# A decayed-attention and two-MoE kernel on one core: attention blocks loaded four ahead, weights' pieces one a block, decay tables made in turn

## Chip, core and metric

The kernel runs on one core of one Trainium2 chip. The metric is device time in microseconds (us) of one execution. Times stand as the median of the runs; the profile is one execution apart from them.

## What is computed

```python
def reference(q, k, v, moe_w_in, moe_w_out, moe2_w_gate, moe2_w_val, moe2_w_out):   # q, k, v: 2 x 8 x 768 x 64
    gamma = 1 - 2.0 ** (-5 - arange(8))
    for t in range(768):                               # retention: a linear attention with decay
        state = gamma * state + outer(k[t], v[t])
        y[t] = q[t] @ state / 8
    x = y as 1536 tokens x 512
    h = x @ moe_w_in                                   # 512 x 2048
    x = (h * tanh(log1p(exp(h)))) @ moe_w_out          # 2048 x 512
    return (sigmoid(x @ moe2_w_gate) * (x @ moe2_w_val)) @ moe2_w_out   # 512 x 1536, 1536 x 512
```

All is fp32 in and out. The weights come as 64-bit words.

## The kernel before

**Attention** runs over 12 blocks of 128 tokens (`NSUB`; 6 of each sequence, `SPB`). Of each block `load(j)` (L449) brings q and k, features first, in one transfer (`qk_t`, 512 KB), and k and v, tokens first, in another (`nv_t`, 512 KB), into rings of three buffers (`ld`, L440). `at_scores(j)` (L461) makes the scores on PE (16 matmul passes into two PSUM banks `sc`), the scaled values `vp` on POOL, and on DVE the two masked scores `a`. `fin(j)` (L518) is `at_state`, which adds the block to the state `st` and lets ACT copy it to `s` for the next block, and `at_out`, which forms the output `ao` from `a` and `vp` and, but for the first block of a sequence, from `s`. DVE then writes `ao` times a decay table `og` into `acc` (L498). The table of a block's place in its sequence is made by POOL from the first one (L473) in the first sequence, kept in six tiles and used again in the second.

**Dense work.** Four blocks are a chunk of 512 tokens. PE multiplies numbers that were split into a high and a low part, three matmuls for each product (`mm3`, L105). So each operand is first split by `split` (L88): ACT copies the high part, DVE or POOL subtracts for the low one. The first chunk's operand is `xc`, made by `put_plain` (L222), the second's are `B11` and `B21`, made by `put_block` (L226): four ACT copies and four DVE differences of 128x512 each. `plain1` (L393) gives dense steps of 12 matmuls with N = 512 on these operands; behind each Mish on ACT and the split of its result `g` (difference on POOL).

**Weights.** A piece is 512 KB (`raw`, three buffers, `stg`). `load_piece` (L129) issues the next one; `pump` (L202) takes the next step of a plan: decode a piece (`decode`, L92: one ACT step, then a TENSOR_SCALAR and two SCALAR_TENSOR_TENSOR on DVE) and `put` it (L158), which copies the high part on ACT and appends the low part's difference to the list `late`; the next pump or the next `weight` empties that list. One dense step calls one pump behind it (`seq`, L379).

**Order.** Until `early.clear()` (L555) every engine follows the order in which the program is written (`InOrder`, L52, records the calls; hence L65 on the profile's rows of this part). Behind it a scheduler orders the instructions. The part in program order is:

```python
for j in range(j0, j0 + SPC):
    if j + 1 < NSUB:
        at_scores(j + 1)
    fin(j)
    load(j + 3)
    load_piece()
    if dense:
        dense.pop(0)()
    if j < SPC:
        pump()
```

once over blocks 0 to 3 with no dense steps, then `put_plain()`, then over blocks 4 to 7 with four dense steps of the first chunk, then `put_block` twice, then over blocks 8 to 11 with the four dense steps of the second chunk (L548 to L554). Ahead of it three blocks and two pieces are loaded (L543 to L547). Behind it come `out1_first` (L403), the sums of operands (L230), and the main loops over weight pairs.

Of the kernel before, what the change touches and what calls it, by code (L numbers as in the profile page):

```python
# [9 lines left out]
F32 = mybir.dt.float32  # L10
# [4 lines left out]
ALU = mybir.AluOpType  # L15
PSUM = bass.MemoryType.PSUM

P = 128
# [4 lines left out]
def kernel(ctx, tc, qk, nv, w1i, w1o, w2g, w2v, w2o, ma_in, og_in, sg_in, ck_in, out):  # L23
# [14 lines left out]
    NP = KK  # L38
    D = P // 2
# [4 lines left out]
    SPC = N // P  # L44
    SPB = NSUB // 2
    RING = 10
    STG = 3
    WARM = 6

    early = [True]  # L50

# [19 lines left out]
    pe, dve, act, pool, sync = [InOrder(e) for e in (nc.tensor, nc.vector, nc.scalar, nc.gpsimd, nc.sync)]  # L71
# [14 lines left out]
    acc_t = [big.tile([P, KK, N], F32, name=f"acc{c}") for c in range(NCH)]  # L86
# [31 lines left out]
    for j in range(FF2 // 2):  # L118
        f = 2 * j
# [6 lines left out]
    steps, late, sums_t, vs = [], [], {}, {}  # L126
    lo_eng = {"w": dve, "g": pool}

    def load_piece():  # L129
        n = cnt["dma"]  # L130
        if n >= len(pieces) or n >= cnt["raw"] + STG:
            return
        kind, i = pieces[n]
        t = stg.tile([P, DM], I64, tag="raw", name="raw")
        sync.dma_start(out=t, in_=src[kind][i])
        raws.append(t)
        cnt["dma"] += 1
# [61 lines left out]
                    ("s", *key, n), sums_t[key][:, 2 * n:2 * n + 2].rearrange("p a b -> p (a b)"))))  # L199
        return True  # L200

    def pump(n=1):  # L202
        while late:
            late.pop(0)()
        for _ in range(n):
            if not steps and not plan():
                return
            if steps[0][0] and not room() or steps[0][0] == 0 and "dcs" not in lo_eng:
                return
            steps.pop(0)[1]()  # L210

    def weight(key):
        while key not in w_t:
            if not steps:
                assert plan(), key
            steps.pop(0)[1]()
        while late:
            late.pop(0)()
        return w_t[key]


    def put_plain():  # L222
        for kk in range(KK):
            split(acc_t[0][:, kk], xc_t[:, kk, 0], xc_t[:, kk, 1], dve)

    def put_block(n, c, k0, eng=None):  # L226
        for k in range(2):
            split(acc_t[c][:, k0 + k], b_t[n][:, k, 0], b_t[n][:, k, 1], eng or dve)
# [150 lines left out]
    def seq(ss, end=None):  # L379

        def step(n):
            ss[n]()
            if n == len(ss) - 1 and end:
                end()
            pump()

        return [lambda n=n: step(n) for n in range(len(ss))]

# [4 lines left out]
    def plain1(i, c=0):  # L393
        ss, r = plain_steps((1, i), (None, ("B11", "B21"), ("T4", "B22"))[c])

        def end(m):
            if m and c == 2:
                dead.update({("a", 1, i, 0), ("a", 1, i, 1)})
            mish(r["c"][m], (1, 2 * i + m, c))

        return [f for m in range(2) for f in seq([ss[m]], lambda m=m: end(m))]
# [35 lines left out]

    with ExitStack() as actx:
        ac = actx.enter_context(tc.tile_pool(name="ac", bufs=1))
        ld = actx.enter_context(tc.tile_pool(name="ld", bufs=3))  # L440
        at = actx.enter_context(tc.tile_pool(name="at", bufs=2))
        ps_s = actx.enter_context(tc.tile_pool(name="ps_s", bufs=1, space=PSUM))
        ma = ac.tile([P, 1, P], F32, name="ma")
        ck = ac.tile([P, SPB, 2 * NP, 1], F32, name="ck")
        sg = ac.tile([P, SPB, NP, 1], F32, name="sg")
        og = [ac.tile([P, NP, P], F32, name=f"og{b}") for b in range(SPB)]
        qk_t, nv_t, a_t, vp_t, st_t, s_t = {}, {}, {}, {}, {}, {}

        def load(j):  # L449
            if j < NSUB:  # L450
                qk_t[j] = ld.tile([P, 2, NP, P], F32, tag="qk", name="qk_t")
                sync.dma_start(out=qk_t[j], in_=qk[j])
                nv_t[j] = ld.tile([P, 2, 2 * NP, D], F32, tag="nv", name="nv_t")
                sync.dma_start(out=nv_t[j], in_=nv[j])
                if j == 0:
                    sync.dma_start(out=ck, in_=ck_in)
                    sync.dma_start(out=ma, in_=ma_in)
                    sync.dma_start(out=og[0], in_=og_in)
                    sync.dma_start(out=sg, in_=sg_in)

        def at_scores(j):  # L461
            t = qk_t[j]
            sc = [ps_h.tile([P, NP, P], F32, tag="h", name="sc") for _ in range(2)]
            for p in range(NP):
                for e in range(2):
                    r = slice(D * e, D * e + D)
                    pe.matmul(out=sc[e][:, p, :], lhsT=t[r, 1, p, :], rhs=t[r, 0, p, :])
            vp_t[j] = at.tile([P, 2 * NP, D], F32, tag="vp", name="vp")
            pool.tensor_tensor(
                out=vp_t[j], in0=nv_t[j][:, 1], in1=ck[:, j % SPB].to_broadcast([P, 2 * NP, D]), op=ALU.mult  # L470
            )
            if 0 < j < SPB:
                pool.tensor_tensor(out=og[j], in0=og[0], in1=sg[:, j].to_broadcast([P, NP, P]), op=ALU.mult)  # L473
            a = at.tile([P, 2, NP, P], F32, tag="a", name="a")
            for e in range(2):
                dve.tensor_tensor(out=a[:, e], in0=sc[e], in1=ma.to_broadcast([P, NP, P]), op=ALU.mult)
            a_t[j] = a

        def at_out(j):
            a, v, t, s = a_t.pop(j), vp_t[j], qk_t[j], s_t.get(j)  # L480
            o = ps_o.tile([P, NP, P], F32, tag="o", name="ao")
            inter = j % SPB > 0

            for p in range(NP):
                for e in range(2):
                    pe.matmul(
                        out=o[D * e:D * e + D, p, :], lhsT=v[:, 2 * p + e, :], rhs=a[:, e, p, :],
                        start=p == 0, stop=p == NP - 1 and not inter, skip_group_check=True,
                    )
            if inter:  # L490
                for p in range(NP):
                    for e in range(2):
                        r = slice(D * e, D * e + D)
                        pe.matmul(
                            out=o[r, p, :], lhsT=s[r, p, :], rhs=t[r, 0, p, :], start=False, stop=p == NP - 1,
                            skip_group_check=True,
                        )
            dve.tensor_tensor(  # L498
                out=acc_t[j // SPC][:, :, j % SPC * P:j % SPC * P + P], in0=o, in1=og[j % SPB], op=ALU.mult
            )  # L500

        def at_state(j):
            if j % SPB == SPB - 1:
                return
            v, k = vp_t[j], nv_t[j]
            if j % SPB == 0:
                st_t[0] = ps_s.tile([P, NP, D], F32, tag="s", name="st")
            st = st_t[0]
            for p in range(NP):
                for e in range(2):  # L510
                    pe.matmul(
                        out=st[D * e:D * e + D, p, :], lhsT=k[:, 0, 2 * p + e, :], rhs=v[:, 2 * p + e, :],
                        start=j % SPB == 0 and p == 0, stop=p == NP - 1, skip_group_check=True,
                    )
            s_t[j + 1] = at.tile([P, NP, D], F32, tag="s", name="s")
            act.activation(out=s_t[j + 1], in_=st, func=AF.Copy)

        def fin(j):  # L518
            at_state(j)
            at_out(j)  # L520

        def blocks(j0, dense):

            for j in range(j0, j0 + SPC):
                if j + 1 < NSUB:
                    at_scores(j + 1)
                fin(j)
                load(j + 3)
                load_piece()
                if dense:  # L530
                    dense.pop(0)()
                if j < SPC:
                    pump()
            run(dense)

        dve.memset(ap=one_t, constant=1.0)
        act.activation(out=sig, in_=one_t, func=AF.Mish)
        z = ac.tile([P, NP * D], F32, name="z")
        dve.memset(ap=z, constant=0.0)
        for n in range(WARM):  # L540
            o = ps_o.tile([P, NP * D], F32, tag="o", name="warm")
            pe.matmul(out=o, lhsT=z[:, 0:P], rhs=z)
        load(0)  # L543
        load(1)
        load(2)
        load_piece()
        load_piece()  # L547
        at_scores(0)  # L548
        blocks(0, [])
        put_plain()  # L550
        blocks(SPC, plain1(0) + plain1(1))
        put_block("B11", 1, 0)
        put_block("B21", 1, 2)
        blocks(2 * SPC, plain1(0, 1) + plain1(1, 1))  # L554
        early.clear()  # L555

    big2 = ctx.enter_context(tc.tile_pool(name="big2", bufs=1))
    up = ctx.enter_context(tc.tile_pool(name="up", bufs=4))
# [35 lines left out]
    for j in range(NG):  # L594
        f = 2 * j
# [62 lines left out]
```

## Time and profile before

| | |
|---|---|
| median of 3 runs | 609.68 us (607.5 to 610.08) |
| the profiled execution | 610.06 us, of which its span is 608.3 |
| busy PE, DVE, POOL, ACT | 587.5 us (97%), 420.3 (69%), 325.2 (53%), 249.8 (41%) |
| mean granted clock of PE | 0.989 |
| chain that ended last | PE 74%, DVE 16%, DMA 2%, ACT 2%, POOL 2%, issue 2% |
| moved by DMA | 52.27 MB, mean 86 GB/s |

Times on rows are in us from the span's start unless marked ns. An engine's row tells in brackets how long it sat idle before it and what ended that. PE's passes are counted: an fp32 matmul of the attention part is two instructions. A granted clock of 1.00 is 2.4 GHz, 0.50 is 1.2 GHz; a mean between them is time at either.

### The profile page before, as it was taken

To read this page: it belongs to the slowest core of one execution; us is meant where nothing else is said; L and a number is where in the kernel's file an instruction comes from. 1 tells how busy PE (TensorE), PEld (TensorE's weight loads), DVE (VectorE), ACT (ScalarE), POOL (GpSimd) and SP (SyncE) were. 2 spreads that over 40 slices of the span, in tenths; PEclk is the share of its full clock that TensorE was granted. 3 is DMA by queue.
4 is the path that set the end of the run, shared out by engine and by line. 5 is a ranking of instruction groups with operands and counts; after the bars stand their busy time and mean duration, and the time that the engine had idled before them with its cause. 6 is when DMAs were issued, how large, how long until landed. Compare 5 with 4: busy or idle time off the path is not lost.

```text
span 608.3 us, 7961 instructions
## 1 busy us (share of the span) xinstructions
PE 587.5 (97%) x3056; PEld 480.6 (79%) x3056; DVE 420.3 (69%) x572; ACT 249.8 (41%) x433; POOL 325.2 (53%) x263
## 2 busy tenths in 40 slices
PE   7789899999999999998999999999999999999997
PEld 6667688888788788886788787888888888888885
DVE  3978799409786676746775985687487587473554
ACT  1243454445454452452434645642334343333210
POOL 3424149326877665574741567755467557457200
PEclk9889899999999999998999999999999999999999
DMA  9866322103231213312021022233023123100014
GB/s 346 324 248 216 139 70 78 62 1 105 73 101 56 84 34 105 105 35 69 36 69 36 1 70 70 70 103 103 1 71 99 41 69 104 35 1 1 1 52 157
DMA packets 15591, 52.27 MB, mean 86 GB/s; under 512 B 1984, under 2 KB 2112, under 8 KB 15552
## 3 DMA queue, kind: packets, MB, share of 16 engines
q1 hardware_dynamic: 15552, 51.75, 24.9%
q8 instruction: 24, 0.39, 0.3%
q14 instruction: 15, 0.12, 0.1%
HBM read 48.60 MB, written 3.15 MB: 85 GB/s over the span
## 4 chain that ended last, share of the span: by engine, by line
PE 74%; DVE 16%; DMA 2%; ACT 2%; POOL 2%; issue 2%; SPq 0%; DVEq 0%; ACTq 0%
PE o L108 31%; PE h L108 28%; PE hx L108 7%; PE h L65 4%; DVE v L101 3%; PE ao L65 2%; DVE v L102 2%; DVE v L100 2%; DVE acc L354 2%; DMA qk_t<-qk 2%; DVE v L65 1%; PE sc L65 1%; POOL w L162 1%; POOL g L90 1%; DVE T L90 1%
## 5 line engine op out<-in xcount | busy, mean ns | idle before, releaser
L90 POOL TENSOR_TENSOR g<-e,g 128x512 fp32r<-128x512 f32 x72 | 103.1, 1441 | 83.4 <-ACT g L89 83.4
L108 PE MATMUL o<-g,w 128*128 128x512 f32 x576 | 141.3, 394 | 2.9 <-DVE acc L354 2.7
L108 PEld LDWEIGHTS o<-g,w 128*128 128x128 f32 x576 | 108.6, 190 | 28.2 <-DVE acc L354 5.0
L108 PE MATMUL h<-T,w 128*128 128x512 f32 x444 | 112.3, 390 | 1.0 <-DVE T L90 0.6
L162 POOL TENSOR_TENSOR w<-v,w 128x512 fp32r<-128x512 f32 x56 | 76.2, 1369 | 67.2 <-ACT w L161 67.0
L108 PE MATMUL o<-w,g 128*128 128x512 f32 x432 | 106.0, 389 | 0.0
L108 PEld LDWEIGHTS h<-T,w 128*128 128x128 f32 x444 | 83.2, 188 | 19.4 <-DVE T L90 1.0
L108 PEld LDWEIGHTS o<-w,g 128*128 128x128 f32 x432 | 81.0, 188 | 17.1 <-POOL g L90 0.4
L108 PE MATMUL h<-B,w 128*128 128x512 f32 x336 | 87.8, 390 | 0.8 <-DVE e L344 0.8
L354 DVE TENSOR_TENSOR acc<-o,acc 128x512 f32<-128x512 f32 x72 | 49.1, 686 | 38.4 <-PE o L108 38.1
L108 PEld LDWEIGHTS h<-B,w 128*128 128x128 f32 x336 | 62.9, 188 | 14.4 <-DVE e L344 1.2
L89 ACT ACTIVATE g<-e 128x512 fp32r<-128x512 f32 x76 | 47.6, 631 | 52.6 <-DVE e L344 35.1
L162 POOL TENSOR_TENSOR w<-s,w 128x512 fp32r<-128x512 f32 x34 | 47.9, 1415 | 35.2 <-ACT w L161 35.0
L374 DVE TENSOR_TENSOR acc<-o,acc 128x512 f32<-128x512 f32 x60 | 41.1, 687 | 30.7 <-PE o L108 30.3
L161 ACT ACTIVATE w<-v 128x512 fp32r<-128x512 f32 x58 | 36.1, 630 | 62.6 <-DVE v L102 34.7
L100 DVE TENSOR_SCALAR v<-v 128x512 int32<-128x512 int32 x58 | 44.4, 767 | 23.2 <-ACT v L99 22.9
L99 ACT ACTIVATE v<-raw 128x512 f32<-128x512 f32 x58 | 38.6, 670 | 49.7 <-POOL w L162 20.0
L102 DVE SCALAR_TENSOR_TENSOR v<-raw,v 128x512 int32<-128x512 int32 x58 | 57.0, 984 | 0.5
L101 DVE SCALAR_TENSOR_TENSOR v<-raw,v 128x512 int32<-128x512 int32 x58 | 56.4, 973 | 1.1
L108 PE MATMUL hx<-xc,w 128*128 128x512 f32 x216 | 55.6, 389 | 0.0
L108 PE MATMUL h<-xc,w 128*128 128x512 f32 x216 | 54.8, 389 | 0.0
L108 PEld LDWEIGHTS hx<-xc,w 128*128 128x128 f32 x216 | 40.6, 188 | 8.4
(78 smaller groups left out, 632.8 us busy)
## 6 DMA issues: line engine op xcount, KB each, us to landing
raw<-w1i SPq DMA_DIRECT2D x16, 512.0 KB, 3.4
raw<-w1o SPq DMA_DIRECT2D x16, 512.0 KB, 3.8
qk_t<-qk SPq DMA_DIRECT2D x12, 512.0 KB, 4.4
nv_t<-nv SPq DMA_DIRECT2D x12, 512.0 KB, 5.5
raw<-w2g SPq DMA_DIRECT2D x12, 512.0 KB, 3.3
raw<-w2v SPq DMA_DIRECT2D x12, 512.0 KB, 3.4
raw<-w2o SPq DMA_DIRECT2D x12, 512.0 KB, 3.4
out<-acc SPq DMA_DIRECT2D x12, 256.0 KB, 2.0
```

Of the source, the lines that this page charges most:

```text
L65: i = call(**kw)
L89: act.activation(out=hi, in_=raw, func=AF.Copy)
L90: eng.tensor_tensor(out=lo, in0=raw, in1=hi.bitcast(F32), op=ALU.subtract)
L99: act.activation(out=v, in_=high.bitcast(F32), func=AF.Copy, scale=2.0 ** -112)
L100: dve.tensor_scalar(out=b, in0=b, scalar1=3, scalar2=None, op0=ALU.logical_shift_left)
L101: dve.scalar_tensor_tensor(out=b, in0=low, scalar=29, in1=b, op0=ALU.logical_shift_right, op1=ALU.bitwise_or)
L102: dve.scalar_tensor_tensor(out=b, in0=high, scalar=SIGN, in1=b, op0=ALU.bitwise_and, op1=ALU.bitwise_or)
L108: pe.matmul(out=o, lhsT=w(a), rhs=x(b), start=first and n == 0, stop=last and n == 2, skip_group_check=more)
L161: act.activation(out=hi, in_=v, func=AF.Copy)
L162: late.append(lambda: lo_eng["w"].tensor_tensor(out=lo, in0=v, in1=hi.bitcast(F32), op=ALU.subtract))
L354: dve.tensor_tensor(out=acc, in0=o, in1=acc, op=ALU.add)
L374: dve.tensor_tensor(out=acc, in0=o, in1=acc, op=ALU.add)
```

## The change

Four attention blocks are loaded ahead in place of three blocks and two pieces, into rings of four buffers (`AHEAD`). In a block the order becomes: next scores, `pump` (from block 3 on), `fin`, `load`, `load_piece`, at a chunk's last block the making of the next chunk's operand (`made`), the low part of the weight (`flush`), the dense step. A dense step of the ordered part no longer pumps. The decay tables other than the first are made by POOL in both sequences, into a ring of two (`og_t`), and the warm-up operand `z` lies in a ring's buffer.

```diff
+    AHEAD = 4
...
+    def flush():
         while late:
             late.pop(0)()
+
+    def pump(n=1):
+        flush()
...
-            pump()
+            if not early:
+                pump()
...
-        ld = actx.enter_context(tc.tile_pool(name="ld", bufs=3))
+        ld = actx.enter_context(tc.tile_pool(name="ld", bufs=AHEAD))
...
-        og = [ac.tile([P, NP, P], F32, name=f"og{b}") for b in range(SPB)]
+        og0 = ac.tile([P, NP, P], F32, name="og0")
...
-            if 0 < j < SPB:
-                pool.tensor_tensor(out=og[j], in0=og[0], in1=sg[:, j].to_broadcast([P, NP, P]), op=ALU.mult)
+            og_t[j] = og0
+            if j % SPB:
+                og_t[j] = at.tile([P, NP, P], F32, tag="og", name="og")
+                pool.tensor_tensor(out=og_t[j], in0=og0, in1=sg[:, j % SPB].to_broadcast([P, NP, P]), op=ALU.mult)
...
-        def blocks(j0, dense):
+        def blocks(j0, dense, made):
 
             for j in range(j0, j0 + SPC):
                 if j + 1 < NSUB:
                     at_scores(j + 1)
+                if j >= SPC - 1:
+                    pump()
                 fin(j)
-                load(j + 3)
+                load(j + AHEAD)
                 load_piece()
+                if j == j0 + SPC - 1:
+                    made()
+                flush()
                 if dense:
                     dense.pop(0)()
-                if j < SPC:
-                    pump()
             run(dense)
...
-        z = ac.tile([P, NP * D], F32, name="z")
+        z = at.tile([P, NP * D], F32, tag="s", name="z")
...
-        load(0)
-        load(1)
-        load(2)
-        load_piece()
-        load_piece()
+        for j in range(AHEAD):
+            load(j)
         at_scores(0)
-        blocks(0, [])
-        put_plain()
-        blocks(SPC, plain1(0) + plain1(1))
-        put_block("B11", 1, 0)
-        put_block("B21", 1, 2)
-        blocks(2 * SPC, plain1(0, 1) + plain1(1, 1))
-        early.clear()
+        blocks(0, [], put_plain)
+        blocks(SPC, plain1(0) + plain1(1), lambda: (put_block("B11", 1, 0), put_block("B21", 1, 2)))
+        blocks(2 * SPC, plain1(0, 1) + plain1(1, 1), early.clear)
```

On SP the transfers that follow block 1's stood so before (`qk_t` and `nv_t` are an attention block's two transfers, `raw` a weight's piece):

```order
L65 DMA qk_t_139<-qk 128x1024
L65 DMA nv_t_141<-nv 128x1024
L65 DMA raw_143<-w1i 128x512
L65 DMA raw_145<-w1i 128x512
L65 DMA qk_t_199<-qk 128x1024
L65 DMA nv_t_201<-nv 128x1024
L65 DMA raw_203<-w1i 128x512
L65 DMA qk_t_256<-qk 128x1024
```

and stand so now:

```order
L66 DMA qk_t_134<-qk 128x1024
L66 DMA nv_t_136<-nv 128x1024
L66 DMA qk_t_138<-qk 128x1024
L66 DMA nv_t_140<-nv 128x1024
L66 DMA qk_t_195<-qk 128x1024
L66 DMA nv_t_197<-nv 128x1024
L66 DMA raw_199<-w1i 128x512
L66 DMA qk_t_246<-qk 128x1024
```

The first piece moved from behind block 2 to behind block 4, and one piece stands between two blocks from there on.

On DVE, from block 4's masked scores to the first operand `xc` and block 5's masked scores, before (`v` is a decoded piece, `w` a weight's low part):

```order
L65 TENSOR_TENSOR a_341<-sc_328,ma_102 128x512
L65 TENSOR_TENSOR a_341<-sc_329,ma_102 128x512
L65 TENSOR_TENSOR acc0_87<-ao_354,og3_108 128x4x128
L65 TENSOR_TENSOR w_326<-v_321,w_326 128x512
L65 TENSOR_SCALAR v_379<-v_379 128x512
L65 SCALAR_TENSOR_TENSOR v_379<-raw_260,v_379 128x512 x2
L65 TENSOR_TENSOR xc_86<-acc0_87,xc_86 128x512 x4
L65 TENSOR_TENSOR a_407<-sc_394,ma_102 128x512
```

and now:

```order
L66 TENSOR_TENSOR a_317<-sc_303,ma_102 128x512
L66 TENSOR_TENSOR a_317<-sc_304,ma_102 128x512
L66 TENSOR_SCALAR v_320<-v_320 128x512
L66 SCALAR_TENSOR_TENSOR v_320<-raw_199,v_320 128x512 x2
L66 TENSOR_TENSOR acc0_87<-ao_337,og_264 128x4x128
L66 TENSOR_TENSOR xc_86<-acc0_87,xc_86 128x512 x4
L66 TENSOR_TENSOR w_325<-v_320,w_325 128x512
L66 TENSOR_TENSOR a_384<-sc_370,ma_102 128x512
```

The decode moved from between `acc` and `xc` to ahead of `acc`, and the weight's low part from ahead of `xc` to behind it.

On ACT, around the second operand, before (`e` is Mish, `g` the copy of its result, `v` a decode's first step, `w` a weight's high part, `s` the state's copy):

```order
L65 ACTIVATE s_626<-st_550 128x256
L65 ACTIVATE e_666<-h_652 128x512
L65 ACTIVATE g_668<-e_666 128x512
L65 ACTIVATE v_671<-raw_507 128x512
L65 ACTIVATE w_676<-v_671 128x512
L65 ACTIVATE B11_84<-acc1_88 128x512 x2
L65 ACTIVATE B21_85<-acc1_88 128x512 x2
L65 ACTIVATE s_709<-st_550 128x256
```

and now:

```order
L66 ACTIVATE v_599<-raw_426 128x512
L66 ACTIVATE w_604<-v_599 128x512
L66 ACTIVATE s_614<-st_536 128x256
L66 ACTIVATE B11_84<-acc1_88 128x512 x2
L66 ACTIVATE B21_85<-acc1_88 128x512 x2
L66 ACTIVATE e_662<-h_649 128x512
L66 ACTIVATE g_664<-e_662 128x512
L66 ACTIVATE v_684<-raw_491 128x512
L66 ACTIVATE w_689<-v_684 128x512
L66 ACTIVATE s_699<-st_536 128x256
```

The copies of `B11` and `B21` moved from behind block 7's Mish and decode to ahead of them, and a block's state copy now stands behind its weight copy.

## Rows read from the trace of the kernel before

**Rows 1.** Stretches: us; busy PE, PEld, DVE, ACT, POOL; granted clock; DMA share; GB/s

```profile
38.00:60.12 22.12, 22.12 (x261) 18.05 (x260) 18.50 (x24) 9.55 (x17) 9.70 (x8) 0.98 0.62 217
62.86:67.50 4.64, 4.64 (x14) 3.17 (x14) 4.64 (x8) 1.78 (x4) 0.00 (x0) 0.66 0.56 225
```

**Rows 2.** Waits of PE, 85.4 us to the end: total us, times, longest

```profile
PE o L108 <- DVE acc L354: 2.7, 3, 2.3
```

**Rows 3.** Time line of PE, blocks 1 to 4: start, us, what, idle before

```profile
13.07 1.09 PE L65 MATMUL ao<-qk_t,s 64*64 64x128 f32 x16
17.08 1.16 PE L65 MATMUL sc<-qk_t 64*128 64x128 f32 x16 [2.92 <-DMA qk_t<-qk]
...
22.27 1.16 PE L65 MATMUL sc<-qk_t 64*128 64x128 f32 x16
...
24.85 1.09 PE L65 MATMUL ao<-qk_t,s 64*64 64x128 f32 x16
...
29.95 1.09 PE L65 MATMUL ao<-qk_t,s 64*64 64x128 f32 x16
```

**Rows 4.** Time line, the first operand and the first two dense products

```profile
32.62 2.18 ACT L65 ACTIVATE xc<-acc 128x512 fp32r<-128x512 f32 x4
33.27 2.50 DVE L65 TENSOR_TENSOR xc<-acc,xc 128x512 fp32r<-128x512 f32 x4 [1.22 <-ACT xc L65]
...
33.29 0.50 PE L65 MATMUL h<-xc,w 128*128 128x512 f32 x1 [2.24 <-ACT xc L65]
...
34.01 4.02 PE L65 MATMUL h<-xc,w 128*128 128x512 f32 x11 [0.23 <-DVE xc L65]
...
41.43 3.01 PE L65 MATMUL h<-xc,w 128*128 128x512 f32 x12
```

**Rows 5.** Time line of PE, the second operand's first product

```profile
62.86 4.63 PE L65 MATMUL h<-B,w 128*128 128x512 f32 x12 [2.74 <-ACT B L65]
```

**Rows 6.** Time line, transfers issued by SP and what they released

```profile
6.95 0.39 SPq L65 DMA_DIRECT2D qk_t<-qk  x1
...
10.48 0.97 PEld L65 LDWEIGHTS sc<-qk_t 64*128 64x128 f32 x16 [0.17 <-DMA qk_t<-qk]
...
13.02 0.67 ACT L65 ACTIVATE v<-raw 128x512 f32<-128x512 f32 x1 [2.91 <-DMA raw<-w1i]
```

**Rows 7.** DMA issues between 5 and 10 us: KB, us to landing

```profile
qk_t<-qk SPq DMA_DIRECT2D x1, 512.0 KB, 10.0
```

**Rows 8.** Groups by form, 38 to 60.12 us: busy us, mean ns, idle before

```profile
L65 DVE SCALAR_TENSOR_TENSOR v<-raw,v 128x512 int32<-128x512 int32 x7 | 7.7, 1105 | 0.2
L65 DVE TENSOR_SCALAR v<-v 128x512 int32<-128x512 int32 x4 | 4.2, 1051 | 3.4 <-ACT v L65 3.4
L65 DVE TENSOR_TENSOR a<-sc,ma 128x512 f32<-128x512 f32 x6 | 3.8, 682 | 0.0
L65 DVE TENSOR_TENSOR acc<-ao,og 128x512 f32<-128x512 f32 x3 | 2.0, 680 | 0.0
...
L65 ACT ACTIVATE w<-v 128x512 fp32r<-128x512 f32 x3 | 1.9, 632 | 9.9 <-DVE v L65 9.9
L65 ACT ACTIVATE s<-st 128x256 f32<-128x256 f32 x2 | 0.7, 366 | 0.0
```

**Rows 9.** Time line of POOL and DVE, 10 to 16 us

```profile
10.21 1.04 POOL L65 TENSOR_TENSOR og<-og,sg 128x512 f32<-128x512 f32 x1
...
13.72 0.46 DVE L65 TENSOR_SCALAR v<-v 128x512 int32<-128x512 int32 x1 [2.43 <-ACT v L65]
14.21 1.42 DVE L65 SCALAR_TENSOR_TENSOR v<-raw,v 128x512 int32<-128x512 int32 x2
```

**Rows 10.** Time line behind the blocks, 90 to 140 us

```profile
91.34 11.14 POOL L65 TENSOR_TENSOR g<-e,g 128x512 fp32r<-128x512 f32 x1 [3.62 <-ACT g L65]
...
107.36 5.60 PE L108 MATMUL o<-g,w 128*128 128x512 f32 x24
...
137.55 0.69 DVE L284 TENSOR_TENSOR u<-h,s 128x512 f32<-128x512 f32 x1 [24.03 <-PE h L108]
```

More of the change, by code (lines that the diff above doesn't have):

```diff
@@ L200, in plan @@
         return True
-    def pump(n=1):
+    def flush():
         while late:
             late.pop(0)()
+    def pump(n=1):
+        flush()
         for _ in range(n):
@@ L216, in weight @@
             steps.pop(0)[1]()
-        while late:
-            late.pop(0)()
+        flush()
         return w_t[key]
@@ L445 @@
         sg = ac.tile([P, SPB, NP, 1], F32, name="sg")
-        og = [ac.tile([P, NP, P], F32, name=f"og{b}") for b in range(SPB)]
-        qk_t, nv_t, a_t, vp_t, st_t, s_t = {}, {}, {}, {}, {}, {}
+        og0 = ac.tile([P, NP, P], F32, name="og0")
+        qk_t, nv_t, a_t, vp_t, og_t, st_t, s_t = {}, {}, {}, {}, {}, {}, {}
         def load(j):
@@ L457, in load @@
                     sync.dma_start(out=ma, in_=ma_in)
-                    sync.dma_start(out=og[0], in_=og_in)
+                    sync.dma_start(out=og0, in_=og_in)
                     sync.dma_start(out=sg, in_=sg_in)
@@ L498, in at_out @@
             dve.tensor_tensor(
-                out=acc_t[j // SPC][:, :, j % SPC * P:j % SPC * P + P], in0=o, in1=og[j % SPB], op=ALU.mult
+                out=acc_t[j // SPC][:, :, j % SPC * P:j % SPC * P + P], in0=o, in1=og_t[j], op=ALU.mult
             )
@@ L526, in blocks @@
                     at_scores(j + 1)
+                if j >= SPC - 1:
+                    pump()
                 fin(j)
-                load(j + 3)
+                load(j + AHEAD)
                 load_piece()
+                if j == j0 + SPC - 1:
+                    made()
+                flush()
                 if dense:
                     dense.pop(0)()
-                if j < SPC:
-                    pump()
             run(dense)
```

## Prediction, on record before the changed kernel ran

> **What bounds the kernel now.** I read the stretches first. From 38.0 to 60.1 us PE (the matmul engine) is busy all the time; from 62.9 to 67.5 it is busy too, but at a mean granted clock of 0.66, so in part at 1.2 GHz in place of 2.4 [rows 1]. Behind 85.4 us the largest sort of wait on PE comes to 2.7 us, 2.3 of them in one place [rows 2]. So what can be won at the start lies before 85.4 us, and PE's order there is the same in both kernels; only its waits can change.
>
> PE's time line shows three of them. Before block 3's scores it idles 2.92 us for that block's q/k, and the attention-only part lasts until 31.0 us [rows 3]. Before the first dense product (weights times `xc`) it idles 2.24 us for ACT, and the product then lasts until 38.0 [rows 4]. Before the first product with `B11` it idles 2.74 us; that product takes 4.63 us, where the same 12 matmuls take 3.01 at full clock [rows 4, 5]. It waits for ACT both times, and idles, then runs slowly.
>
> **Transfers.** SP's queue lands in the order of issue: block 2's q/k releases PE at 10.5 us and the first weight piece releases ACT at 13.0; that is two transfers of 512 KB (block 2's k/v is the other), 1.27 us each [rows 6]. Block 3's q/k was issued at 6.95 and took 10.0 us, to 16.95 [rows 6, 7]: two pieces stood ahead of it, 2.5 us. By the pace it should have landed at 10.5 + 4 x 1.27 = 15.6; 1.4 us stay unexplained. After the change no piece is ahead of it: block 3's q/k at 10.5 + 2 x 1.27 = 13.0, block 4's at 15.6, block 5's, behind one piece, at 19.4; with the unexplained 1.4 us at 14.4, 17.0 and 20.8. PE wants them at 14.2, 17.8 and 21.5 (next part), so it waits for a transfer 0.2 us at most. Behind that 3 x 1.27 = 3.8 us of transfers stand against 6.65 us of PE a block.
>
> **Blocks 2 to 4.** PE ends block 1's output at 13.07 + 1.09 = 14.16. One undisturbed round of scores, state and two output products goes from 22.27 to 25.94, 3.67 us [rows 3]. Three of them: 14.16 + 3 x 3.67 = 25.2, where before has 31.0: 5.8 us.
>
> **The first operand.** `put_plain` now stands at the end of block 3, ahead of block 5's masks and of the next decode; PE has block 5's scores and block 4's state and output (3.67 us) between block 3's `acc` and the product. But a decode (`pump`) now stands ahead of that `acc`. The chain, with the durations of [rows 4, 8, 9]: block 4's scores end at 17.8 + 1.16 = 19.0; DVE's two masks, 2 x 0.68, to 20.4; the decode, undisturbed (0.49 from its start to the next one's, then 1.42), to 22.3; ACT's weight copy 0.63 and state copy 0.37, to 23.3; DVE's four differences start 0.65 behind ACT's first copy and take 2.50, to 26.5; the low half of the weight, now behind them, 0.62 (a quarter of the 2.50), to 27.1. PE is free at 25.2 and runs two matmuls; the third needs that low half. Ten matmuls of 0.25 then end at 29.6, where before has 38.0: **8.4 us**, the 5.8 of the last part among them. Bounds: without this wait 25.2 + 3.0 = 28.2, 9.8 us; with the lower clock again, 4.63 - 3.01 = 1.6 less, 6.8 us.
>
> **Blocks 5 to 7** are 22.1 us of unbroken PE in both [rows 1]; each weight is made one block ahead of its use.
>
> **The second operand.** `B11` and `B21` are made at the end of block 7, and PE again has 3.67 us of block 8 between: the 2.74 and the slow 1.6 go, **4.4 us**. What is late next: on ACT a block's state copy now stands behind its weight copy, which waits for DVE's decode; B stands behind both, and Mish and the next decode's first step behind B. DVE's round is masks 1.36, decode 1.05 + 2 x 1.10, `acc` 0.68, low half 0.62, together 5.9 us [rows 8], against PE's 3.67 + 3.01 = 6.7. The table products, five more of 1.04 us on POOL [rows 9], add a collision a block: the two last steps of a decode took 1.42 undisturbed and 2 x 1.10 beside one POOL product [rows 8, 9], so 0.8 more: as much as PE. In block 7 the four differences come on top. From the end of block 7's `acc`: 0.65 + 2.50, low half 0.62, masks 1.36, decode 3.25 to 4.05, copies 1.0, so block 8's state copy is there after 9.4 to 10.2 us. Walking DVE's rounds of 5.9 to 6.7 us from 27.1 on beside PE's of 6.7 from 29.6 on (each decode behind the dense step before it, as ACT's order has it), that `acc` ends some 1.2 us after PE's dense step of block 7, an estimate; from that step PE needs 3.67 + 3.01 + 2.6 = 9.3 until it wants the copy. PE waits 1.3 to 2.1 us; I take **1.5**, since masks and `acc` of the blocks before can run ahead. Bounds: 0, if POOL's products fall beside masks and `acc`; 2.1 + 1.6 = 3.7 with the lower clock.
>
> That POOL and DVE hold each other up is in [rows 8, 9]. The Trainium skill ("SBUF — State Buffer", section "SBUF: two separate sides") speaks against the new products more strongly: a VectorE instruction with two SBUF inputs and a GpSimd instruction exclude each other, and the loser stands still for the whole of the other. By it a table product costs DVE its full 1.04 in place of the rows' 0.8, five times, and the sum would be some 1.2 us higher.
>
> **Edits at nothing.** The warm-up tile in another pool and `og0` as a tile of its own move no instruction on the path. One pump fewer in the blocks moves one piece's decode (3.9 us of DVE with its low half) behind them, beside 20 us of queued PE work; if that cover goes, it is rival 2. Behind the blocks the order of PE differs for some 35 us, then all is as before.
>
> **Sum.** 610.06 (the profiled execution; the median of the runs shown, 609.68, is 0.06% lower) - 8.4 - 4.4 + 1.5 = **598.8 us**. With all bounds at their best 610.06 - 9.8 - 4.4 = 595.9, at their worst 610.06 - 6.8 - 4.4 + 3.7 = 602.6.
>
> **Rivals.**
> (1) DVE becomes the bound of blocks 7 to 11. If every POOL product blocks DVE for its length, a round is 0.49 + 1.42 + 0.62 of DVE beside nothing, 3 x 1.04 of POOL and 2.04 of masks and `acc`: 7.7 us against 6.7. Five blocks lose 5.0 and the four differences 2.5: 610.06 - 12.8 + 7.5 = 604.8. For it: the decode is stretched in every block [rows 8]. Against: masks and `acc`, which read PSUM, take 0.68 there as everywhere, and POOL can run beside them. The page named above would make it so.
> (2) Slower: POOL is shut out. At 91.3 us one difference on POOL took 11.14 us while DVE ran without a gap; it ended at 102.5, and PE wanted it at 107.4 [rows 10], so it was hidden. After the change DVE carries one piece more there. If DVE leaves no gap until its backlog is done (in before at 137.55 - 24.03 = 113.5 [rows 10], 28 us behind the blocks; now 3 us more), POOL's two last differences land 33 us behind the blocks; PE wants them at 22. That is 11 us and two slow stretches, 3.2: 610.06 - 11.3 + 14.2 = 613.0. It takes the whole gain if they land later than 30 us behind the blocks. Against: in before DVE let POOL in after 17 us.
> (3) The change does not do to the transfers what it says: the unexplained part is more, and block 3 still lands at 17 us. PE then loses 2.8 and the slow clock 1.6: 603.2.
>
> **Chances.** The forecast 0.65 (595.9 to 602.6), rival 1 0.20 (602.6 to 607), rival 3 0.10, rival 2 0.05. The range takes in the forecast's bounds, most of rival 1 and 1 us below, since the lower clock may also give back more than was counted: 595 to 606. A measurement of this kernel can tell about 0.5% from no change, 3 us: faster than that is 0.91 (the forecast, rival 3, and eight tenths of rival 1), the same 0.05 (the rest of rival 1 and the mildest of rival 2), slower 0.04.
>
> **What would show it.** Right: no wait of PE for q/k behind 10.5 us; the first dense product begun near 25 and ended near 29.6, with a wait inside that DVE's low half ends; no wait for ACT's B; blocks over near 74 us in place of 85.4; later waits as before. Wrong: DVE busy for 95% and more from 40 to 74 us while PE idles for the state copy or the masks in several blocks (rival 1); PE idling for POOL's difference some 20 us behind the blocks (rival 2); PE waiting for block 3's q/k until 17 us (rival 3).

## The result, and the profile after

The changed kernel takes **603.26 us** (median of 4 runs, 603.13 to 603.4), the kernel before, run beside it, 608.73 us (4 runs, 607.5 to 610.08). The ratio is 0.991, with a 95% interval of 0.9884 to 0.9936: faster by 5.5 us. The profiled execution took 603.4 us against 610.06, 6.7 us less. Forecast were 598.8 us and a gain of 11.3: the direction and the range hold, but the time is 4.6 us off, and only about half of the gain came.

The page of the changed kernel begins with these lines, among others; the last is the clock granted to PE in 40 slices.

```profile
span 601.6 us, 7973 instructions
...
PE 585.4 (97%) x3056; PEld 478.6 (80%) x3056; DVE 416.0 (69%) x572; ACT 249.5 (41%) x433; POOL 331.5 (55%) x268
...
PEclk9999899999999999998999999999999999999999
```

PE's instructions are as many as before; the 6.7 us are idle time and time at the lower clock. The waits of PE over the whole span, after (what waits, for what, us in total, times, longest):

```profile
PE st L66 <- issue: 4.0, 3, 2.4
PE o L109 <- DVE acc L357: 2.6, 3, 2.3
...
PE sc L66 <- DMA qk_t<-qk: 0.6, 1, 0.6
PE hx L109 <- ACT e L341: 0.6, 2, 0.3
```

The waits that the change was to remove are gone: those for q/k [rows 3], of which one of 0.6 us for block 1 is left, the one for the first operand [rows 4] and the one for B [rows 5]. The wait behind the blocks [rows 2] is as it was. New is the first line: the state product `st` waits three times, 4.0 us in all, for "issue", that is, for nothing the profile names. PE's time line after, in the rows that answer to [rows 3, 4, 5] and those of the new waits:

```profile
14.17 1.16 PE L66 MATMUL sc<-qk_t 64*128 64x128 f32 x16
...
17.77 1.16 PE L66 MATMUL sc<-qk_t 64*128 64x128 f32 x16
...
21.37 1.16 PE L66 MATMUL sc<-qk_t 64*128 64x128 f32 x16
23.19 0.69 PE L66 MATMUL st<-vp,nv_t 128*64 128x64 f32 x16 [0.66 <-issue]
...
25.70 0.73 PE L66 MATMUL h<-xc,w 128*128 128x512 f32 x2
27.26 2.59 PE L66 MATMUL h<-xc,w 128*128 128x512 f32 x10 [0.82 <-DVE w L66]
...
43.49 0.69 PE L66 MATMUL st<-vp,nv_t 128*64 128x64 f32 x16 [0.93 <-issue]
...
52.61 3.01 PE L66 MATMUL h<-B,w 128*128 128x512 f32 x12
...
59.11 0.69 PE L66 MATMUL st<-vp,nv_t 128*64 128x64 f32 x16 [2.40 <-issue]
...
60.76 1.97 PE L66 MATMUL ao<-qk_t,s 64*64 64x128 f32 x16
62.66 3.54 PE L66 MATMUL h<-B,w 128*128 128x512 f32 x12
...
77.58 5.60 PE L109 MATMUL o<-g,w 128*128 128x512 f32 x24
```

Blocks 3 to 5 now follow every 3.6 us, where the kernel before waited up to 2.92 us [rows 3]; the first dense product begins at 25.70, and the first with B takes 3.01 us without a wait, where it took 4.63 behind one of 2.74 [rows 5]. The last row is the first product behind the blocks; it stood at 85.60 us before. So **8.0 us were won up to there**. Of these 6.8 are left at 136 us (DVE's sum `acc`, at 142.89 before, begins at 136.10), and from there on both kernels run alike. Inside the blocks PE stands still twice more, at 43.49 and 59.11. Behind the second wait it is slow, as the stretch from 60.76 to 62.70 shows (length; busy PE; granted clock; DMA share; GB/s):

```profile
60.76:62.70 1.94, 1.94 (x19) 0.50 0.04 15
```

A granted clock of 0.50 is 1.2 GHz. PE had idled 2.40 us just before. What ended that idle time stands on ACT. ACT, DVE and POOL after, at the first operand, at the state copy of block 6 (43.02) and in block 8:

```profile
22.19 0.63 ACT L66 ACTIVATE w<-v 128x512 fp32r<-128x512 f32 x1 [1.97 <-DVE v L66]
...
22.73 0.36 ACT L66 ACTIVATE s<-st 128x256 f32<-128x256 f32 x1
22.99 2.18 ACT L66 ACTIVATE xc<-acc 128x512 fp32r<-128x512 f32 x4
...
23.64 2.96 DVE L66 TENSOR_TENSOR xc<-acc,xc 128x512 fp32r<-128x512 f32 x4 [0.88 <-ACT xc L66]
...
26.52 0.68 DVE L66 TENSOR_TENSOR w<-v,w 128x512 fp32r<-128x512 f32 x1
...
43.02 0.36 ACT L66 ACTIVATE s<-st 128x256 f32<-128x256 f32 x1
...
55.22 2.86 DVE L66 SCALAR_TENSOR_TENSOR v<-raw,v 128x512 int32<-128x512 int32 x2
...
56.05 1.48 POOL L66 TENSOR_TENSOR og<-og,sg 128x512 f32<-128x512 f32 x1
...
58.11 0.63 ACT L66 ACTIVATE w<-v 128x512 fp32r<-128x512 f32 x1 [4.33 <-DVE v L66]
...
58.65 0.37 ACT L66 ACTIVATE s<-st 128x256 f32<-128x256 f32 x1
```

The copies of the state `s` end at 22.73 + 0.36 = 23.09, at 43.38 and at 59.02. The three waiting `st` products begin 0.10, 0.11 and 0.09 us behind that. `st` adds into the PSUM tile that ACT still has to read, so it waits for the copy of the block before. And the copy stands on ACT behind the weight copy `w`, before which ACT sat idle for 4.33 us until DVE's decode was done. The decode's last two steps are stretched to 2.86 us by POOL's products beside them; undisturbed they take 1.42 [rows 9].

### The profile page after: what moved, and what is told of

Same layout as the page of the kernel before. It is cut to its first block, busy times and chain, and to the rows that moved or that the text cites. A ratio compares the mean times of both kernels' runs of the same rounds, so it can differ in the third digit from the quotient of the medians.

```text
span 601.6 us, 7973 instructions
## 1 busy us (share of the span) xinstructions
PE 585.4 (97%) x3056; PEld 478.6 (80%) x3056; DVE 416.0 (69%) x572; ACT 249.5 (41%) x433; POOL 331.5 (55%) x268
## 4 chain that ended last, share of the span: by engine, by line
PE 64%; DVE 15%; issue 7%; POOL 6%; DMA 4%; ACT 3%; SPq 0%; POOLq 0%; ACTq 0%; DVEq 0%
PE o L109 29%; PE h L109 27%; PE hx L109 7%; DVE v L102 3%; DMA nv_t<-nv 3%; DVE v L103 2%; DVE v L101 2%; DVE acc L357 2%; POOL w L163 1%; POOL vp L66 1%; POOL g L91 1%; DVE v L66 1%; POOL og L66 1%; POOL g L66 1%; DVE T L91 1%
## 5 line engine op out<-in xcount | busy, mean ns | idle before, releaser
L91 POOL TENSOR_TENSOR g<-e,g 128x512 fp32r<-128x512 f32 x73 | 116.5, 1605 | 86.7 <-ACT g L90 86.7
L109 PE MATMUL h<-B,w 128*128 128x512 f32 x348 | 90.8, 390 | 0.8 <-DVE e L347 0.8
L109 PEld LDWEIGHTS h<-B,w 128*128 128x128 f32 x348 | 65.1, 188 | 15.1 <-DVE e L347 1.2
```

Of the source, the lines that this page charges most:

```text
L91: eng.tensor_tensor(out=lo, in0=raw, in1=hi.bitcast(F32), op=ALU.subtract)
L109: pe.matmul(out=o, lhsT=w(a), rhs=x(b), start=first and n == 0, stop=last and n == 2, skip_group_check=more)
```

## The experiments

The theory from here on: the order on ACT, state copy behind weight copy, makes `st` wait; the stretched decode sets how long. Rivals: DVE's amount of work sets the end whatever the order; and the gain has another source than the forecast says. Each kernel starts from the changed one, and each ratio is to the kernel before, run beside it: 608.95 us (12 runs) for the state ahead alone, the tables left out alone, the operand made late, and the loads alone; 609.68 us (15 runs) for the other four.

**The state ahead of the weight.** `at_state` and so the state copy go ahead of the decode, `at_out` stays behind it.

```diff
+                at_state(j)
                 if j >= SPC - 1:
                     pump()
-                fin(j)
+                at_out(j)
```

> Edit: the changed kernel, but a block's state (its products and ACT's copy) is issued ahead of the weight piece's decode and copy, not behind. In the changed kernel the state products of blocks 4, 7 and 9 started 0.66, 0.93 and 2.40 us late, each right behind ACT's copy of the state before, and the slow clock followed the last (1.6 us). Theory A (the copy stands behind the weight's copy on ACT, which waits for DVE's decode): these waits go, the ordered part ends at 72.5 to 73.5 us in place of 77.6, the time is 598 to 600. Theory B (DVE's work bounds blocks 7 to 11 and the copy only shows it): PE waits as long elsewhere (masks, operands), the part ends at 76.5 or later, the time is 602 or more.

Measured: 601.18 us (6 runs), ratio 0.9878 (0.985 to 0.9907); the blocks end at 74.62 us. Both lie between the two expectations. No `st` waits any more. Two stretches of PE's time line of this kernel, at the first dense product and behind the blocks:

```profile
27.41 4.15 PE L66 MATMUL h<-xc,w 128*128 128x512 f32 x10 [1.72 <-DVE w L66]
...
74.62 2.88 PE L109 MATMUL o<-g,w 128*128 128x512 f32 x12
...
77.79 3.02 PE L109 MATMUL o<-g,w 128*128 128x512 f32 x12 [0.29 <-DVE acc L66]
...
81.94 3.02 PE L109 MATMUL o<-g,w 128*128 128x512 f32 x12 [0.45 <-ACT acc L365]
...
97.05 1.65 PE L109 MATMUL hx<-T,w 128*128 128x512 f32 x6 [1.20 <-ACT e L341]
```

The wait for the state goes, as the theory says, and although the first dense product now waits 1.72 us for the weight's low part (0.82 before this edit) and runs slowly behind it, the blocks end 3.0 us earlier (74.62 against 77.58). But PE waits again behind them, for DVE and ACT, and of the 3.0 us only 0.9 are left at 135 us (`acc` at 135.25 against 136.10). So the rival is right for what comes next: DVE's work, which POOL's products stretch, is the second limit, hidden behind the first (the next two experiments test it).

**No tables in the second sequence.** POOL's five products there are left out (blocks 7 to 11).

```diff
-            if j % SPB:
+            if 0 < j < SPB:
```

> Edit: the changed kernel without the five table products of the second sequence (its blocks take the first table, so their values differ). Theory A (order on ACT): each decode of blocks 6 to 10 is shorter by 0.7 us, so the copy of block 6 comes 0.7 earlier and that of block 8 1.4 earlier, the waits shrink to about 0.2 and 1.0 and the slow clock may go: the ordered part ends at 74 to 76 us, the time is 600 to 602. Theory B (DVE and POOL bound blocks 7 to 11): five times 0.7 and the slow clock go, the part ends near 72.5, the time is 598.5 or less.

Measured: 598.58 us (4 runs), ratio 0.9837 (0.9799 to 0.9875), 4.7 us under the changed kernel. Its `st` waits and first product behind the blocks, and one pair of decode steps:

```profile
42.61 0.69 PE L66 MATMUL st<-vp,nv_t 128*64 128x64 f32 x16 [0.23 <-issue]
...
56.80 0.69 PE L66 MATMUL st<-vp,nv_t 128*64 128x64 f32 x16 [1.02 <-issue]
...
73.70 5.60 PE L109 MATMUL o<-g,w 128*128 128x512 f32 x24
```

```profile
53.62 2.14 DVE L66 SCALAR_TENSOR_TENSOR v<-raw,v 128x512 int32<-128x512 int32 x2
```

The waits shrink from 0.93 and 2.40 to 0.23 and 1.02 us with the order untouched, as expected, no slow stretch follows, and the 3.9 us at the blocks' end are kept behind them. The end and the time are better than the 74 to 76 and 600 to 602 us of the theory; the time lies at the edge of the rival's. The price of a table product is seen on DVE's groups by shape from 40 to 72 us (count; busy us, mean ns; idle before), first of the changed kernel, then of this one:

```profile
L66 DVE SCALAR_TENSOR_TENSOR v<-raw,v 128x512 int32<-128x512 int32 x10 | 14.1, 1412 | 0.3
```

```profile
L66 DVE SCALAR_TENSOR_TENSOR v<-raw,v 128x512 int32<-128x512 int32 x11 | 11.2, 1021 | 0.4
```

A step takes 1.41 us in place of 1.02; a pair beside two POOL products takes 2.86 us, beside one 2.14, alone 1.42. So each product costs DVE 0.72 us where it collides.

**Both together.** State first, and no tables in the second sequence.

> Edit: state ahead of the decode, and the second sequence's table products left out (its blocks take the first table, so their values differ). Theory C: the two add up; PE waits at no state product, only inside the first dense product (1.7 us, with or without the slow clock), block 11's dense step is over at 72.5 to 74.5 us, nothing is given back behind it; the time is 596.5 to 598.5. Theory B alone (DVE and POOL decide, the order on ACT nothing): no better than without the products alone, 598.6 us give or take 0.7.

Measured: 596.62 us (4 runs), ratio 0.9802 (0.9775 to 0.983): less than with either alone, though the interval overlaps that of the tables alone. The time lines are plainer: the first product behind the blocks begins 1.3 us sooner than without the tables alone, and 2.2 us sooner than with the state first alone.

```profile
72.44 5.60 PE L109 MATMUL o<-g,w 128*128 128x512 f32 x24
```

Order and load are two limits, one behind the other.

**The operand made late.** `made()` goes behind the dense step, where the operands were made before.

```diff
-                if j == j0 + SPC - 1:
-                    made()
...
             run(dense)
+            made()
```

> Edit: the changed kernel, but the next chunk's operand is made behind the chunk's last dense step, as before the change; the rest is as changed. If making it ahead of the dense step is what freed PE from ACT's B (the prediction's 4.4 us): PE idles 2 to 3 us for B again with the slow clock behind it, the ordered part ends near 82 us, the time is near 607. If it was the decode's move from between the dense step and B to ahead of the block's output: B comes within 0.5 us of PE's need, the state copy of block 8 comes 0.7 later, the part ends at 77.5 to 78.5, the time is 603 to 604.5. The first operand does not move (there is no dense step ahead of it), but for the weight's low part, which is now ahead of it: the first dense product waits 0.6 us less.

Measured: 604.36 us (5 runs), ratio 0.9919 (0.989 to 0.9949); 1.1 us from the changed kernel, less than the spread of its own runs (602.13 to 605.11). The first product behind the blocks begins at 77.45 against 77.58 us. B costs PE two short waits, and the next `st` waits less:

```profile
54.37 0.96 PE L66 MATMUL h<-B,w 128*128 128x512 f32 x3 [0.49 <-DVE B L66]
...
60.39 0.69 PE L66 MATMUL st<-vp,nv_t 128*64 128x64 f32 x16 [2.06 <-issue]
```

The equal end is in part luck: behind that wait this execution had no slow stretch (its mean granted clock is 1.000, and it is the fastest of the five), where the changed kernel lost 1.6 us at the lower clock. So the place of the making may be worth up to some 1.6 us, an estimate from that difference, but not the 4.4 of the forecast.

**Loads and tables alone.** Four blocks ahead and tables in turn, but the decode behind the dense step and the operand behind the chunk, as before.

```diff
-                if j >= SPC - 1:
-                    pump()
                 fin(j)
...
-                if j == j0 + SPC - 1:
-                    made()
-                flush()
                 if dense:
                     dense.pop(0)()
+                if SPC - 1 <= j < NSUB - 1:
+                    pump()
             run(dense)
+            made()
```

> Edit: of the change the transfers (four blocks ahead, one piece a block), the tables in turn and the first pump in block 3 alone; a block's order is as before the change (output, dense step, then pump; operand behind the loop). Theory A (the loads are worth the waits for q/k with their slow clock and what they delay, 5.8 us; the order of decode and operand the rest): PE waits for no q/k behind 10.5 us, but 2 to 3 us for xc and 2.7 for B, with the slow clock behind each; no wait at the state products; the ordered part ends at 79 to 80.5 us, the time is 604.5 to 606.5. Rival (the loads alone do all of it): the part ends at 77.6 or earlier, the time is 603.3 or less.

Measured: 628.96 us (4 runs), ratio 1.033 (1.0295 to 1.0366): 20 us slower than before, outside both expectations. PE's time line of this kernel, at two of its dense products and the first product behind the blocks:

```profile
31.63 4.00 PE L66 MATMUL h<-xc,w 128*128 128x512 f32 x10 [3.70 <-DVE w L66]
...
80.14 5.79 PE L66 MATMUL h<-B,w 128*128 128x512 f32 x12 [3.46 <-ACT B L66]
...
104.67 5.15 PE L109 MATMUL o<-g,w 128*128 128x512 f32 x22
```

The kernel before decoded a piece in each of blocks 0 to 3 and was always ahead. Here decoding starts in block 3, since no piece is there sooner, and each weight comes just before its use: each of the first five dense steps has waits of 3 us and more, and a slow stretch. So the early loads pay only together with the decode moved ahead of a block's output, or with an earlier decode, which was not tried. The parts of this change don't add.

**Two pieces ahead again.** The changed kernel with two weight pieces issued in front of block 3's loads.

```diff
         for j in range(AHEAD):
+            if j == AHEAD - 1:
+                load_piece()
+                load_piece()
             load(j)
```

> Edit: the changed kernel, but two weight pieces stand ahead of block 3 in SP's queue, as before the change. The prediction's term (2.5 us of transfers ahead of block 3, a wait of PE with the slow clock behind it): block 3's q/k lands 2.5 us later, PE idles 2 to 3 us before its scores, the slow clock adds up to 1.6, all of it on the path: o's first product at 80 to 82 us, the time 605.5 to 608. Rival (the later waits absorb it, since the weights' pieces come earlier): first product at 78.5 or earlier, the time below 604.5.

Measured: 605.49 us (10 runs), ratio 0.9931 (0.991 to 0.9952): 2.2 us of the gain gone by the medians, though the interval touches that of the changed kernel. What was lost, and where, is plainer in PE's time line of this kernel:

```profile
16.88 1.16 PE L66 MATMUL sc<-qk_t 64*128 64x128 f32 x16 [2.53 <-DMA qk_t<-qk]
...
63.78 0.69 PE L66 MATMUL st<-vp,nv_t 128*64 128x64 f32 x16 [2.38 <-issue]
...
66.29 3.03 PE L66 MATMUL h<-B,w 128*128 128x512 f32 x12
...
80.83 5.60 PE L109 MATMUL o<-g,w 128*128 128x512 f32 x24
```

Block 3's q/k is late again, by 2.53 us where the kernel before had 2.92 [rows 3]; with the slow stretch behind it, block 4's scores come 4.3 us later than in the changed kernel (22.07 against 17.77), and the blocks end 3.25 us later, as expected. The transfers' term of the sum is real. The wait for the state in block 9, 2.38 us, is as long as in the changed kernel, but here no slow stretch follows: the dense product behind it takes 3.03 us.

**The tables taken from POOL altogether.** DVE applies the decay itself when it writes `acc`, in four steps of 128x128 with a scalar each.

```diff
-                og_t[j] = at.tile([P, NP, P], F32, tag="og", name="og")
-                pool.tensor_tensor(...)
...
+            for p in range(NP):
+                dve.scalar_tensor_tensor(
+                    out=acc[:, p, :], in0=o[:, p, :], scalar=sg[:, j % SPB, p, :], in1=og0[:, p, :], op0=ALU.mult,
+                    op1=ALU.mult,
+                )
```

> Edit: the changed kernel with only the first of those edits: no table products on POOL, DVE's output step in four of 128x128. If such a step takes 0.2 to 0.25 us, DVE gains 0.4 to 0.6 a block in blocks 7 to 11: waits of the state products near those without the second sequence's products (0.23 and 1.02), o's first product at 74 to 75.5 us, the time 599 to 601. If it takes 0.35 or more, nothing is won: 77.6 or later, 603 or more.

Measured: 598.27 us (4 runs), ratio 0.9818 (0.9791 to 0.9846), as good as leaving the tables out, and a little better than expected.

```profile
47.13 1.12 DVE L66 SCALAR_TENSOR_TENSOR acc<-ao,sg,og 128x128 f32<-128x128 f32 x4
```

The four steps take 1.12 us, 0.44 more than the one they replace (0.68), and cost POOL nothing.

**That, with the state first and the weight's low part ahead of the operand.** The second and third edits:

```diff
+                at_state(j)
                 if j >= SPC - 1:
                     pump()
-                fin(j)
+                at_out(j)
...
+                flush()
                 if j == j0 + SPC - 1:
                     made()
-                flush()
```

> Edit: the changed kernel with three edits: no table products on POOL (DVE writes a block's output in four steps of 128x128, each times a scalar of its place and the first table), a block's state ahead of the decode, and the weight's low part ahead of the next chunk's operand. Theory C (two things cost the 3.3 us that the prediction missed: the state copy's place on ACT, and DVE's time lost to POOL's products, which comes back behind the blocks): no wait at the state products, the wait inside the first dense product goes from 0.8 to 0 or moves to xc, no slow clock; PE is through with block 11's dense step at 71.5 to 73 us and the gain holds behind the blocks; the time is 596 to 598.5. If four small steps cost DVE more than 1.4 us (the one step takes 0.68 and a collision 0.72): 600 or more.

Measured: **595.54 us** (5 runs, 594.24 to 596.1), ratio 0.9777 (0.975 to 0.9805): faster than both kernels, by 14 and by 8 us, and a little faster than expected. Its PE time line from the first dense product on:

```profile
25.26 3.03 PE L66 MATMUL h<-xc,w 128*128 128x512 f32 x12
...
70.93 5.60 PE L109 MATMUL o<-g,w 128*128 128x512 f32 x24
```

Between these rows PE has no idle time: the waits for the weight's low part (0.82 us after the change) and for the state are gone, and the blocks end 6.65 us sooner than in the changed kernel.

Keeping all six tables beside four load buffers wasn't tried.

## Why the prediction was right or wrong

**Transfers: right.** The scores of blocks 3, 4 and 5 begin at 14.17, 17.77 and 21.37 us without a wait; forecast were 14.2, 17.8 and 21.5. Block 3's q/k was issued at 6.01 and took 7.0 us, so it landed at 13.0; block 4's, issued at 7.46, took 9.5 and landed at 17.0. The forecast had 13.0 and 15.6, and 17.0 with the 1.4 us that it left unexplained. Two pieces put back cost 2.53 us at the same place.

**First operand: right in size and in its parts.** The dense product began at 25.70 (forecast 25.2; `st` had waited 0.66 us for the state copy just before), waited inside for the weight's low part, 0.82 us, and ended at 29.78 (29.6): of the 8.4 us, 8.2 came. The forecast's round of 3.67 us is 0.07 too long, since groups on PE's time line overlap a little: blocks follow every 3.60. The chain is as walked, too: DVE's differences end at 23.64 + 2.96 = 26.6 and the low part at 27.2, where 26.5 and 27.1 were forecast.

**Second operand: right in size, not in its cause.** The wait for B and the slow stretch are gone, 4.4 us as forecast. But with the operand made late, and the decode where the change puts it, PE waits for B only 0.49 and 0.48 us; with the decode moved back too, it waits 3.46, though there every weight is late as well. So it is mainly the decode's move that frees ACT and DVE in time, not the operand's. The forecast didn't tell the two edits apart.

**The new wait: right in kind, wrong in place, number and size; this is the step that failed.** The forecast had the state copy wanted by block 9's output product, 9.3 us behind block 7's dense step, and took 1.5 us. In fact `st` of block 9 wants it, because it writes the tile that the copy reads: 1.5 us sooner (in block 10, which doesn't wait, `st` begins at 67.22 and that product at 68.71). DVE was a little faster than walked: the copy ended 59.02 - 48.96 = 10.1 us behind block 7's dense step, which the forecast's terms put at 1.2 + 9.4 = 10.6 to 11.4. So the wait was 2.40 in place of 1.5. By the same need `st` of block 7 waits 0.93 us, where the forecast had none. And the lower clock followed the longer wait: 0.88 + 0.18 + 0.53 = 1.6 us on the three products behind it (1.97, 1.23 and 3.54 us, at full clock 1.09, 1.05 and 3.01); the forecast had it in its bounds alone. It is not a constant: behind the same wait, 2.38 us, the kernel with two pieces ahead ran at full clock. With the 0.2 of the first operand these make 3.6 us, against 3.3 missed (block 6's scores gave back 0.3: 1.49 us before, behind the slow product, now 1.16): the first product behind the blocks was to come at 85.6 - 8.4 - 4.4 + 1.5 = 74.3 and came at 77.58.

**Behind the blocks: wrong.** "Later waits as before" left out 1.2 us. All of it lies at two new waits for ACT's Mish `e`, 0.27 and 0.33 us in the list of waits. From 96.62 to 99.22 us nine matmuls take 2.60 us, and from 105.34 to 108.95 thirteen take 3.61; at the pace of the 24 that begin at 77.58 (5.44 us until the next) they would take 2.04 and 2.95. The difference is 1.2 us, twice the idle time: PE also loses time at both edges of such a wait. Where the first wait comes from stands on POOL and ACT:

```profile
81.66 9.36 POOL L91 TENSOR_TENSOR g<-e,g 128x512 fp32r<-128x512 f32 x1 [6.11 <-ACT g L90]
...
93.95 0.66 ACT L100 ACTIVATE v<-raw 128x512 f32<-128x512 f32 x1 [7.63 <-POOL s L176]
...
97.73 1.65 PE L109 MATMUL hx<-T,w 128*128 128x512 f32 x6 [0.27 <-ACT e L341]
```

One difference on POOL takes 9.36 us while DVE works without a gap until 89.9, POOL's sums `s` stand behind it, ACT idles 7.63 us for the last of them, and Mish stands behind on ACT and begins at 97.09. In the kernel before the sums stood ahead of such a difference. That this chain costs the time is read from the trace; no run isolates it. The chain begins when DVE is through with the blocks, so PE loses by it where DVE comes later than PE. With the state first alone DVE's last `acc` of the blocks begins at 77.06, 2.4 us behind PE's first product behind them, and 2.1 of 3.0 us are lost again; with the tables out it begins at 73.79, 0.1 us behind, and nothing is lost.

**Collision of POOL and DVE: right in size.** Forecast was 0.8 us more for a decode beside a table product, measured are 0.72. The page that the prediction named, the Trainium skill's "SBUF — State Buffer", section "SBUF: two separate sides", has the loser wait for the whole of the other instruction, 1.04 us here. The trace shows less on DVE, 0.72, and POOL's own product stretched from 1.04 to 1.48, so each waits for a part of the other. Whether the two exclude each other in turn or share, no run here tells. What the prediction set against rival 1 holds: the masked scores (two steps from 53.56 to 54.84 us, beside POOL's difference from 53.30 to 54.81) and `acc` (at 10.68, beside a table product from 10.29 to 11.33) still take 0.68 to 0.69 us each.

**Rivals.** Rival 2 didn't come as told: no wait of PE for POOL stands in the list. But POOL was shut out, for 9.36 us, which reached PE by way of ACT and cost at most the 1.2 us above in place of 14.2. Rival 3 didn't come. Rival 1's time, 604.8, is nearer to the profiled 603.4 than the forecast is, but not by its mechanism, in which blocks 7 to 11 would each lose 1.0 us to DVE: in block 8 and from block 10 on PE has no wait at the state. What it had right is that POOL's products are the reason the wait is long; without them in the second sequence the kernel takes 598.6 us, about the time forecast.

## What to carry to other kernels

When work moves on an engine that runs in order, look up for each instruction queued behind it the *first* consumer, and count a writer that reuses the tile as one: here the matmul that adds into a PSUM tile wanted the copy out of it done, before anything read the copy. A copy that frees a tile is better not put behind an instruction that waits for another engine; here that cost up to 2.40 us at a time. And a helper engine isn't free because it is idle: taking POOL's products away and giving DVE 0.44 us more a block was worth 5 us, nearly as much as the whole change.

## What was not expected of the hardware

**The same idle time is not always followed by the lower clock.** Between 266 and 301 us every profile has one wait of PE of 2.28 or 2.29 us for DVE, followed by the same 54 matmuls. First this row of the changed kernel, then that of the kernel with the operand made late:

```profile
274.37 14.13 PE L109 MATMUL o<-g,w 128*128 128x512 f32 x54 [2.28 <-DVE acc L357]
```

```profile
274.73 12.53 PE L109 MATMUL o<-g,w 128*128 128x512 f32 x54 [2.29 <-DVE acc L357]
```

The first runs at a mean granted clock of 0.83 over 10 us, the second at 1.00. In the ten profiles it went the one way five times (13.95 to 14.15 us) and the other way five times (12.53 to 12.58): a difference of 1.4 to 1.6 us. No edit touches this place, and the executions of one kernel differ as well: the ten of the kernel with two pieces ahead go from 603.39 us at a mean clock of 1.000 to 607.04 at 0.994. What decides it stays open. It is the same for the wait of 1.72 us ahead of the first dense product, behind which ten matmuls take 4.15 us in the state-first kernel and 2.55 in the one that also leaves out tables. A forecast should carry such a stretch as a chance, not as a constant.
